# Where the transposed loads of x stand on SyncE's queue, and what TensorE does between K's first pieces

## The chip, the cores and the metric

One NeuronCore of a Trainium2 chip runs the whole kernel. The metric is the device time of one execution in microseconds (us), as the median of several runs. Beside it stands one profiled execution, whose trace gives every instruction's start and duration.

## The reference, cut to what matters

x is 2048 x 640 in bf16. A gate mixes a linear-attention block with an MLP whose first layer shifts channels along the sequence:

```
q, k, v = split(x @ wqkv)                       # 32 heads of 20
phi(t)  = where(t > 0, t + 1, exp(t)) + 1e-6
a  = (phi(q) @ (phi(k)^T v)) / (phi(q) . sum_s phi(k) + 1e-6) @ wo
h  = gelu(layernorm(x) @ w1)                    # four groups of channels shifted by 1, -1, 2, -2
x1 = x + shifted(h) @ w2
b  = x1 + gelu(layernorm(x1) @ w3) @ w4
g  = sigmoid(sum(x * gate_w))
out = g * a + (1 - g) * b
```

## The kernel before, in words

The order on every engine is the order of the program text (a manual schedule); the framework only adds the semaphore waits. The 2048 rows of x are 16 chunks of 128 rows; the 640 columns are five blocks of 128 (index dc). The stages follow one another on TensorE: K for each chunk (L185), Q in ten units (L242), the product of phi(k) and x (L319), the layers of the MLP and the attention output.

K of a chunk needs xT, x transposed, in SBUF, as the weights of ten matmuls (five blocks dc, two halves of the output), and wk, the K columns of wqkv. Chunks 0 and 1 are transposed on TensorE: turn(c) (L207) multiplies x by an identity into PSUM (L215 for chunk 0, L213 for chunk 1), and VectorE copies the result to xT (L218), blocks 0 and 1 first, then 2 to 4. Chunks 2 to 15 are transposed by DMA: load_xT (L122) issues a DMA transpose from DRAM on SyncE's queue (L123).

The gate's dot product rides along in K: wk_sb has one more column, filled with gate_w. L217 is a small matmul that turns gate_w into that layout, and L221 copies it to wk_sb. The second half of every K piece has 321 columns and reads it.

The loads are issued at the start of the program (L128 to L147). On SyncE: x chunk 0, wk blocks 1, 3 and 4, then the six transposes (chunks 2, 3, 4-5, 6-7, 8-11, 12-15), wq (L138, into the memory of hsT), the other chunks of x (L139, by L120), wv, w1, wo, w2, w3. On ScalarE: gate_w, wk block 0, x chunk 1, wk block 2. Every DMA also waits for the completion counter that it shares with the DMA eight before it.

K of chunk 0 takes its blocks in the order 1, 0, 3, 4, 2, as the wk blocks come in (k0_order, L192). warmup (L196) puts matmuls on a constant, whose results are not used, on TensorE: six while nothing has been loaded yet (L202, L203), one after turn(0) (L224), and one of 256 columns, a filler, between the first and second and between the second and third pieces of K (L229). Ahead of the fourth piece stands turn(1).

GpSimd makes the masks and the identity (L150 to L166) and then w1x, a copy of parts of w1 (L167 to L169), which waits for the load of w1. Its next work is the rstd of the layer norm (L289, L290).

Of the kernel before, what the change touches and what calls it, by code (L numbers as in the profile page):

```python
# [16 lines left out]
def kernel(  # L17
# [13 lines left out]
    nc = tc.nc  # L31
    P = 128
    S, D = A_x.shape[1], A_x.shape[2]
    F = B_w3.shape[1]
    H, Dh = 32, 20
    NCH = S // P
# [3 lines left out]
    DC = D // P  # L40
# [4 lines left out]
    CG = D // 4  # L45
# [4 lines left out]
    NG = 6  # L50
    row0 = [g * GW for g in range(5)] + [D - P]
# [3 lines left out]
    x2 = A_x.rearrange("b s d -> (b s) d")  # L55
    out2 = out.rearrange("b s d -> (b s) d")
    wqkv_v = A_wqkv.rearrange("(c p) f -> p c f", p=P)
# [20 lines left out]
    w1_sb = const.tile([P, DC, D], BF16)  # L78
    w1x = const.tile([P, DC, P], BF16)
    w2_sb = const.tile([P, DC, D], BF16)  # L80
    w3_sb = const.tile([P, DC, F], BF16)
    wo_sb = const.tile([P, NG, D], BF16)
# [21 lines left out]
    wq_sb = hsT[:, :, 0:D]  # L104
    wv_sb = m_sb
# [5 lines left out]
    xT = st1.tile([P, DC, S], BF16)  # L111
# [5 lines left out]
    sp, aq, gq = nc.sync, nc.scalar, nc.gpsimd  # L117

    def load_x(c0, c1, q=sp):
        q.dma_start(x_sb[:, c0:c1, 0:D], x2[c0 * P:c1 * P, :].rearrange("(c p) d -> p c d", p=P))  # L120

    def load_xT(c0, c1):  # L122
        sp.dma_start_transpose(xT[:, :, c0 * P:c1 * P], x2[c0 * P:c1 * P, :])  # L123

    def load_wk(q, dc):
        q.dma_start(wk_sb[:, dc, 0:D], A_wqkv[dc * P:(dc + 1) * P, D:2 * D])
# [6 lines left out]
    load_wk(sp, 3)  # L133
    load_wk(aq, 2)
    load_wk(sp, 4)
    for c0, c1 in ((2, 3), (3, 4), (4, 6), (6, 8), (8, 12), (12, 16)):
        load_xT(c0, c1)
    sp.dma_start(wq_sb, wqkv_v[:, :, 0:D])  # L138
    load_x(2, 16)  # L139
    sp.dma_start(wv_sb[:], wqkv_v[:, :, 2 * D:3 * D])  # L140
    sp.dma_start(w1_sb[:], B_w1.rearrange("(c p) f -> p c f", p=P))
    for g in range(NG):
        sp.dma_start(wo_sb[:, g, :], A_wo[row0[g]:row0[g] + P, :])
    for g in range(4):
        sp.dma_start(w2_sb[:, g, :], B_w2[CG * g:CG * g + P, :])
        sp.dma_start(w2_sb[32 * g:32 * (g + 1), 4, :], B_w2[CG * g + P:CG * (g + 1), :])
    sp.dma_start(w3_sb[:], B_w3.rearrange("(c p) f -> p c f", p=P))  # L147


    nc.gpsimd.memset(mhalf[:], -0.5)  # L150
# [10 lines left out]
    for m, n, off in ((bmask, GH, 0), (bmask5, 2, 88)):  # L161
# [2 lines left out]
                                base=-off, pattern=[[-Dh, n], [0, 4]], channel_multiplier=1)  # L164
        nc.gpsimd.affine_select(out=m[:], in_=m[:], compare_op=ALU.is_ge, fill=0.0,
                                base=off + Dh - 1, pattern=[[Dh, n], [0, 4]], channel_multiplier=-1)  # L166
    for dc in range(DC):  # L167
        for g in range(4):
            nc.gpsimd.tensor_copy(w1x[:, dc, 32 * g:32 * (g + 1)], w1_sb[:, dc, CG * g + P:CG * (g + 1)])  # L169


    def phi(dst, src, n):
# [8 lines left out]
    def k_mm(pt, c, dcs, first=0, last=DC - 1):  # L181
        for dc in dcs:
            for hf in range(2):
                n = HD + hf
                nc.tensor.matmul(pt[:, hf, 0:n], lhsT=xT[:, dc, c * P:(c + 1) * P],  # L185
                                 rhs=wk_sb[:, dc, hf * HD:hf * HD + n], start=(dc == first), stop=(dc == last))
# [9 lines left out]
    def warmup(n, w=TS):  # L196
        for i in range(n):
            nc.tensor.matmul(warm[:, 1, 0:w], lhsT=one[:, 0:P], rhs=one[:, 0:w], start=True, stop=True)  # L198
# [8 lines left out]
    def turn(c):  # L207
        for pt, a, b in turns:
            ptb = pt[:, 0, :].bitcast(BF16) if c else pt[:, 0, :]
            for dc in range(a, b):  # L210
                dst, src = ptb[:, (dc - a) * P:(dc - a + 1) * P], x_sb[:, c, dc * P:(dc + 1) * P]
                if c:
                    nc.tensor.transpose(dst, src, ident[:])  # L213
                else:
                    nc.tensor.matmul(dst, lhsT=src, rhs=ident[:], start=True, stop=True)  # L215
            if c == 0 and b == DC:
                nc.tensor.matmul(pt[:, 1, 0:DC], lhsT=g5z[:], rhs=ident[:, 0:DC], start=True, stop=True)  # L217
            nc.vector.tensor_copy(xT[:, a:b, c * P:(c + 1) * P],  # L218
                                  ptb[:, 0:(b - a) * P].rearrange("p (c s) -> p c s", c=b - a))
            if c == 0 and b == DC:  # L220
                nc.vector.tensor_copy(wk_sb[:, :, D], pt[:, 1, 0:DC])  # L221

    turn(0)
    warmup(1, TS)  # L224
    for n, dc in enumerate(k0_order):
        if n == 3:
            turn(1)
        elif 1 <= n < 3:
            warmup(1, 2 * P)  # L229
        k_mm(kp, 0, (dc,), first=k0_order[0], last=k0_order[-1])  # L230
    k_evac(kp, 0)
    for c in range(1, NCH):
# [414 lines left out]
```

## Time and profile before

| | |
|---|---|
| median of 3 runs | 263.02 us (262.87 to 264.37) |
| the profiled execution's own time | 262.89 us |
| its span, first to last instruction | 261.1 us |
| granted TensorE clock | 1.00 |
| VectorE busy in 0 to 27.2 us (K's stage) | 18.28 us |
| K: first matmul to Q's first matmul | 4.22 to 27.22 us |
| SyncE's last early load (w3) issued | 36.76 us |
| SyncE's next transpose | 54.08 us |

All times in the trace are counted from the start of the span. PE is TensorE's matmuls and PEld its weight loads, which overlap with matmuls; DVE is VectorE, ACT ScalarE, POOL GpSimd, SPq SyncE's queue of DMA issues. A DMA row's duration is the time that its issue takes on the queue, not the transfer. Matmuls are pipelined and their ends are modelled, so two rows can overlap; the distance between two starts is what a matmul costs.

### The profile page before, as it was taken

How to read it: one execution, taken by the hardware profiler on the slowest of the kernel's cores; microseconds unless marked ns; L12 is line 12 of the kernel's file. 1: busy time of each engine (PE TensorE's matmuls, PEld its weight loads, DVE VectorE, ACT ScalarE, POOL GpSimd, SP SyncE). 2: the span in 40 equal slices, each digit the busy share in tenths (PEclk: the TensorE clock that was granted, in tenths of full speed). 3: DMA queues.
4: the chain of work that ended last, by engine and by line, in shares of the span. 5: the costliest groups of instructions: out<-in, count | busy, mean ns of one | idle time of the engine just before them, and what ended most of it. 6: DMA issues, size and time to landing. Idle time of an engine off the chain costs nothing.

```text
span 261.1 us, 4172 instructions
## 1 busy us (share of the span) xinstructions
PE 257.6 (99%) x1670; PEld 159.1 (61%) x1670; DVE 141.9 (54%) x277; ACT 82.9 (32%) x124; POOL 27.1 (10%) x82
## 2 busy tenths in 40 slices
PE   8999999999999999999999999999999999999995
PEld 4777555788754644565676566567745567555543
DVE  2788778899947884967312378970312223112132
ACT  1555554321165346431520311140233350142100
POOL 3000050012220140131000123310000000000000
PEclk9999999999999999999999999999999999999999
DMA  7999987016684826996002011331200001100011
GB/s 205 179 204 377 365 241 306 0 28 126 125 99 88 220 54 145 207 298 60 0 3 75 25 28 25 75 54 25 78 25 0 0 3 50 53 0 0 0 53 50
DMA packets 47265, 25.78 MB, mean 99 GB/s; under 512 B 35214, under 2 KB 46478, under 8 KB 47246
## 3 DMA queue, kind: packets, MB, share of 16 engines
q1 hardware_dynamic: 46804, 25.03, 39.5%
q10 hardware_dynamic: 442, 0.49, 0.5%
q8 instruction: 13, 0.21, 0.4%
q14 instruction: 6, 0.05, 0.1%
HBM read 13.03 MB, written 3.60 MB: 64 GB/s over the span
## 4 chain that ended last, share of the span: by engine, by line
PE 99%; DVE 0%; issue 0%
PE pp L518 22%; PE pp L483 21%; PE pp L185 9%; PE pp L319 8%; PE pp L436 8%; PE pp L467 8%; PE pp L353 8%; PE pp L242 8%; PE pp L198 1%; PE pp L527 1%; PE pp L492 1%; PE pp L386 1%; PE pp L372 1%; PE pp L257 0%; PE pp L215 0%; DVE oc L532 0%
## 5 line engine op out<-in xcount | busy, mean ns | idle before, releaser
L483 PE MATMUL pp<-lnxT,w_sb 128*128 128x512 bf16 x260 | 60.0, 379 | 0.0
L518 PE MATMUL pp<-w_sb,h 128*128 128x384 bf16 (+3 forms) x416 | 57.9, 299 | 0.0
L485 ACT ACTIVATE h<-pp 128x1024 bf16<-128x1024 f32 (+1 forms) x28 | 27.0, 963 | 94.3 <-PE pp L483 94.3
L518 PEld LDWEIGHTS <-h 128*128 128x128 bf16 x416 | 38.3, 98 | 19.4 <-issue 1.2
L483 PEld LDWEIGHTS <-w_sb 128*128 128x128 bf16 x260 | 25.4, 98 | 27.2
L532 DVE SCALAR_TENSOR_TENSOR oc<-pp,omg,x 128x640 bf16<-128x640 f32 (+2 forms) x20 | 14.4, 748 | 45.4 <-PE pp L527 21.2
L470 DVE SCALAR_TENSOR_TENSOR x<-pp,gate,x 128x640 f32<-128x640 f32 x16 | 14.1, 879 | 33.6 <-PE pp L467 33.6
L177 ACT ACTIVATE e<-pp 128x640 bf16<-128x640 f32 (+1 forms) x26 | 21.5, 827 | 9.6 <-PE pp L242 9.6
L467 PE MATMUL pp<-m_sb,pqT 128*128 128x320 bf16 x160 | 24.3, 299 | 0.0
L436 PE MATMUL pp<-w_sb,hsT 128*128 128x320 bf16 x160 | 23.5, 299 | 0.0
L185 PE MATMUL pp<-wk_sb,xT 128*128 128x320 bf16 (+1 forms) x160 | 23.0, 302 | 0.0
L319 PE MATMUL pp<-x_sb,pk 128*128 128x320 bf16 (+1 forms) x160 | 22.0, 300 | 0.0
L242 PE MATMUL pp<-xT,hsT 128*128 128x512 bf16 x100 | 21.7, 379 | 0.0
L319 PEld LDWEIGHTS <-pk 128*128 128x128 bf16 x160 | 18.8, 117 | 3.2
L436 PEld LDWEIGHTS <-hsT 128*128 128x128 bf16 x160 | 15.6, 98 | 7.7
L467 PEld LDWEIGHTS <-pqT 128*128 128x128 bf16 x160 | 15.7, 98 | 7.7
L289 POOL TENSOR_SCALAR rstd<-mv 128x1 f32<-128x1 f32 (+1 forms) x20 | 7.7, 386 | 115.4 <-DVE mv L295 115.4
L185 PEld LDWEIGHTS <-xT 128*128 128x128 bf16 x160 | 15.6, 99 | 6.5 <-DVE xT L218 0.2
L439 DVE TENSOR_TENSOR x<-pp,x_sb 128x640 f32<-128x640 f32 x16 | 13.1, 816 | 10.6 <-PE pp L436 10.4
L353 PE MATMUL pp<-lnxT,w_sb 128*128 128x512 bf16 x80 | 18.1, 379 | 0.0
L242 PEld LDWEIGHTS <-hsT 128*128 128x128 bf16 x100 | 11.8, 118 | 9.7
L179 DVE SCALAR_TENSOR_TENSOR pk<-pp,e 128x640 bf16<-128x640 f32 x16 | 13.2, 825 | 1.7
(75 smaller groups left out, 191.1 us busy)
## 6 DMA issues: line engine op xcount, KB each, us to landing
x_sb<-in_A_x_dram SPq DMA_DIRECT2D x1, 2240.0 KB, 11.2
out_dram<-oc SPq DMA_DIRECT2D x14, 160.0 KB, 1.8
w_sb<-in_B_w_dram SPq DMA_DIRECT2D x1, 2160.0 KB
w_sb<-in_B_w_dram SPq DMA_DIRECT2D x1, 2080.0 KB, 11.7
wo_sb<-in_A_wo_dram SPq DMA_DIRECT2D x6, 160.0 KB, 7.3
m_dram<-x SPq DMA_DIRECT2D x3, 320.0 KB, 2.9
hsT<-in_A_wqkv_dram SPq DMA_DIRECT2D x1, 800.0 KB
m_sb<-in_A_wqkv_dram SPq DMA_DIRECT2D x1, 800.0 KB
```

The costliest lines, as they stand in the source:

```text
L177: nc.scalar.activation(ev, src, ACT.Exp)
L185: nc.tensor.matmul(pt[:, hf, 0:n], lhsT=xT[:, dc, c * P:(c + 1) * P], rhs=wk_sb[:, dc, hf * HD:hf * HD + n], start=(dc == first), stop=(dc ...
L242: nc.tensor.matmul(pt[:, t % 2, :], lhsT=wq_sb[:, dc, :].rearrange("p (m j) -> p j m", j=DC)[:, j], rhs=xT[:, dc, t * TS:(t + 1) * TS], st ...
L319: nc.tensor.matmul(pt[:, hf, 0:HD + hf], lhsT=w, rhs=x_sb[:, c, hf * HD:(hf + 1) * HD + hf], start=(c == 0), stop=(c == NCH - 1))
L353: nc.tensor.matmul(pt[:, i, :], lhsT=w, rhs=lnxT[t][:, dc, :], start=(dc == 0), stop=(dc == DC - 1))
L436: nc.tensor.matmul(pt[:, hf, 0:HD], lhsT=hsT[:, fc, 2 + c * P:2 + (c + 1) * P], rhs=w2_sb[:, fc, hf * HD:(hf + 1) * HD], start=(fc == 0), ...
L467: nc.tensor.matmul(pt[:, hf, 0:HD], lhsT=pqT[:, j, c * P:(c + 1) * P], rhs=m_sb[:, j, hf * HD:(hf + 1) * HD], start=(j == 0), stop=(j == D ...
L470: nc.vector.scalar_tensor_tensor(x1, pt[:, :, 0:HD], gate[:, c:c + 1], x1, op0=ALU.mult, op1=ALU.add)
L483: nc.tensor.matmul(pt[:, k, :], lhsT=w3_sb[:, dc, fc * P:(fc + 1) * P], rhs=lnT[:, dc, :], start=(dc == 0), stop=(dc == DC - 1))
L485: nc.scalar.activation(h2[:, 2 * i * TS:(2 * i + n) * TS], pt[:].rearrange("p h e -> p (h e)")[:, 0:n * TS], ACT.Gelu_apprx_tanh)
L518: nc.tensor.matmul(dst, lhsT=st[t]["h2"][:, fc * TS + cc * P:fc * TS + (cc + 1) * P], rhs=w4_sb[:, fc, a:b], start=start and fc == 0, stop ...
L532: nc.vector.scalar_tensor_tensor(oc[:, a:b], src, omg[:, c:c + 1], st[t]["x1"][cc][:, a:b], op0=ALU.mult, op1=ALU.add)
```

## The change

- The late loads (transposes, wq and all behind it) are put into a function, late_loads, which is called after turn(0) in the program text. SyncE's queue holds the same DMAs in the same order, but the transposes are now one per chunk: 14 instead of 6.
- A new memset on VectorE writes one column of xT in chunk 2, which the first transpose writes too. So the first transpose has to wait for this memset, and all later DMAs of SyncE's queue stand behind it.
- The matmul for the gate column and its copy to wk_sb move from after the second half of turn(0) to after its first half. The memset follows that copy, ahead of the second copy to xT.
- The two fillers between K's pieces are gone.
- GpSimd's copies to w1x move in the text behind late_loads, as they must follow the load of w1. GpSimd's own order stays the same.

The lines of the kernel after are shifted by a few against those of before: L198 becomes L197, L185 becomes L184, L138 becomes L140.

```diff
-    def load_xT(c0, c1):
-        sp.dma_start_transpose(xT[:, :, c0 * P:c1 * P], x2[c0 * P:c1 * P, :])
+    def load_xT(c):
+        sp.dma_start_transpose(xT[:, :, c * P:(c + 1) * P], x2[c * P:(c + 1) * P, :])
...
-    for c0, c1 in ((2, 3), (3, 4), (4, 6), (6, 8), (8, 12), (12, 16)):
-        load_xT(c0, c1)
-    sp.dma_start(wq_sb, wqkv_v[:, :, 0:D])
-    load_x(2, 16)
...
+    def late_loads():
+        for c in range(2, NCH):
+            load_xT(c)
+        sp.dma_start(wq_sb, wqkv_v[:, :, 0:D])
+        load_x(2, 16)
...
-    for dc in range(DC):
-        for g in range(4):
-            nc.gpsimd.tensor_copy(w1x[:, dc, 32 * g:32 * (g + 1)], w1_sb[:, dc, CG * g + P:CG * (g + 1)])
...
-            if c == 0 and b == DC:
+            if c == 0 and a == 0:
                 nc.tensor.matmul(pt[:, 1, 0:DC], lhsT=g5z[:], rhs=ident[:, 0:DC], start=True, stop=True)
             nc.vector.tensor_copy(xT[:, a:b, c * P:(c + 1) * P],
                                   ptb[:, 0:(b - a) * P].rearrange("p (c s) -> p c s", c=b - a))
-            if c == 0 and b == DC:
+            if c == 0 and a == 0:
                 nc.vector.tensor_copy(wk_sb[:, :, D], pt[:, 1, 0:DC])
+                nc.vector.memset(xT[:, 0:1, 2 * P:2 * P + 1], 0.0)
 
     turn(0)
+    late_loads()
+    for dc in range(DC):
+        for g in range(4):
+            nc.gpsimd.tensor_copy(w1x[:, dc, 32 * g:32 * (g + 1)], w1_sb[:, dc, CG * g + P:CG * (g + 1)])
     warmup(1, TS)
     for n, dc in enumerate(k0_order):
         if n == 3:
             turn(1)
-        elif 1 <= n < 3:
-            warmup(1, 2 * P)
         k_mm(kp, 0, (dc,), first=k0_order[0], last=k0_order[-1])
```

More of the change, by code (lines that the diff above doesn't have):

```diff
@@ L135 @@
     load_wk(sp, 4)
-    for c0, c1 in ((2, 3), (3, 4), (4, 6), (6, 8), (8, 12), (12, 16)):
-        load_xT(c0, c1)
-    sp.dma_start(wq_sb, wqkv_v[:, :, 0:D])
-    load_x(2, 16)
[L140 to L143, printed above, removed]
-    for g in range(4):
-        sp.dma_start(w2_sb[:, g, :], B_w2[CG * g:CG * g + P, :])
-        sp.dma_start(w2_sb[32 * g:32 * (g + 1), 4, :], B_w2[CG * g + P:CG * (g + 1), :])
-    sp.dma_start(w3_sb[:], B_w3.rearrange("(c p) f -> p c f", p=P))
+    def late_loads():
[3 more added lines that the diff above has]
+        load_x(2, 16)
+        sp.dma_start(wv_sb[:], wqkv_v[:, :, 2 * D:3 * D])
+        sp.dma_start(w1_sb[:], B_w1.rearrange("(c p) f -> p c f", p=P))
+        for g in range(NG):
+            sp.dma_start(wo_sb[:, g, :], A_wo[row0[g]:row0[g] + P, :])
+        for g in range(4):
+            sp.dma_start(w2_sb[:, g, :], B_w2[CG * g:CG * g + P, :])
+            sp.dma_start(w2_sb[32 * g:32 * (g + 1), 4, :], B_w2[CG * g + P:CG * (g + 1), :])
+        sp.dma_start(w3_sb[:], B_w3.rearrange("(c p) f -> p c f", p=P))
     nc.gpsimd.memset(mhalf[:], -0.5)
@@ L166 @@
                                 base=off + Dh - 1, pattern=[[Dh, n], [0, 4]], channel_multiplier=-1)
-    for dc in range(DC):
-        for g in range(4):
-            nc.gpsimd.tensor_copy(w1x[:, dc, 32 * g:32 * (g + 1)], w1_sb[:, dc, CG * g + P:CG * (g + 1)])
     def phi(dst, src, n):
@@ L219, in turn @@
                                   ptb[:, 0:(b - a) * P].rearrange("p (c s) -> p c s", c=b - a))
-            if c == 0 and b == DC:
+            if c == 0 and a == 0:
                 nc.vector.tensor_copy(wk_sb[:, :, D], pt[:, 1, 0:DC])
+                nc.vector.memset(xT[:, 0:1, 2 * P:2 * P + 1], 0.0)
     turn(0)
+    late_loads()
+    for dc in range(DC):
+        for g in range(4):
+            nc.gpsimd.tensor_copy(w1x[:, dc, 32 * g:32 * (g + 1)], w1_sb[:, dc, CG * g + P:CG * (g + 1)])
     warmup(1, TS)
```

## The prediction

> **What bounds the kernel now.** I read the page first: busy time, then the chain that ended last.
>
> ```profile
> span 261.1 us, 4172 instructions
> PE 257.6 (99%) x1670; PEld 159.1 (61%) x1670; DVE 141.9 (54%) x277; ACT 82.9 (32%) x124; POOL 27.1 (10%) x82
> ...
> PE 99%; DVE 0%; issue 0%
> ```
>
> TensorE carries the whole end. The busy time by stage says the same: 21.80 of 21.8 us in 27.2:49, and 50.00 of 50 in each of the three stages from 100 to 250. So a microsecond that TensorE gains or loses in the first 27 us reaches the end almost whole, and the change acts only there. Hence the next view, the timeline of TensorE in the first 10 us (start, duration, line; the end of a matmul is modelled, so the next start is the safer mark).
>
> ```profile
> 3.23 0.74 PE L215 MATMUL pp<-ident,x_sb 128*128 128x128 bf16 x5
> 3.77 0.21 PE L217 MATMUL pp<-ident,g5z 128*128 128x5 bf16 x1
> 3.84 0.59 PE L198 MATMUL pp<-const-bfloat16-1.0 128*128 128x512 bf16 x1
> 4.22 0.93 PE L185 MATMUL pp<-wk_sb,xT 128*128 128x320 bf16 x2
> 4.94 0.42 PE L198 MATMUL pp<-const-bfloat16-1.0 128*128 128x256 bf16 x1
> 5.15 0.48 PE L185 MATMUL pp<-wk_sb,xT 128*128 128x320 bf16 x2
> 5.47 0.27 PE L198 MATMUL pp<-const-bfloat16-1.0 128*128 128x256 bf16 x1
> 5.58 0.43 PE L185 MATMUL pp<-wk_sb,xT 128*128 128x320 bf16 x2
> 5.85 0.44 PE L213 MATMUL pp<-ident,x_sb 128*128 128x128 bf16 x5
> ```
>
> The two L198 rows at 4.94 and 5.47 are the fillers that go: they take 4.94 to 5.15 and 5.47 to 5.58, 0.32 us together. The second K matmul starts only at 4.72 (same timeline, narrower window), since it waits for the column copy of L221. After this K's fourth piece starts at 6.13 and its fifth at 6.51, though the fourth needs only 2 x 0.136: a gap of 0.11 us, which I read as the last piece of wk arriving.
>
> SyncE's queue, from its timeline:
>
> ```profile
> 2.65 13.64 SPq L123 DMA_TRANSPOSE xT<-in_A_x_dram  x6
> 16.33 0.58 SPq L138 DMA_DIRECT2D hsT<-in_A_wqkv_dram  x1
> ...
> 57.80 5.24 SPq L311 DMA_TRANSPOSE lnxT<-ln  x4
> ```
>
> And the one wait of TensorE on a transpose of x, from the waits (total, times, longest):
>
> ```profile
> PEld L185 <- DMA xT<-in_A_x_dram: 0.2, 1, 0.2
> ```
>
> The six transposes start at 2.65, 3.99, 5.30, 6.74, 8.60 and 12.72. So one chunk alone costs SyncE 1.31 to 1.34 us from start to start, two cost 1.44 to 1.86, four 4.1 and 3.6. The four of L311 give the same 1.31 each. The wait of 0.2 at 16.30 held up a weight load only.
>
> **What the skill says.** "DMA: Bandwidth & Descriptors", section on queues, rings and completion order: each DMA engine takes turns between the queues that have work, packet by packet. That is why a transpose on SyncE's queue can delay a wk piece on ScalarE's; the trace agrees in so far as the rate falls from 371 GB/s (5.0:5.5) to 282 and 149 (5.5:6.0, 6.0:6.5) while wk ends. Same page, latency and other measured facts: a DMA transpose moves 261 GB/s, so by estimate 0.63 us for a chunk of 164 KB, less than the 1.31 us that issuing it takes. The trace doesn't split the two. "TensorE: Matmul & The Clock Gate", Part 1: the full clock comes after a free-running window of about 3.4 us of activity. Here weight loads fall from 151 to 98 ns between 4.2 and 4.7 and matmul steps from 0.27 to 0.13 near 5.1, 4.3 us after the first.
>
> **The change, step by step.**
>
> *Fillers and the column.* L217 moves ahead of three transposes, its copy L221 ahead of the second copy. The first copy now also waits for L217, which starts at about 3.45 and takes 0.11: copy at about 3.70 instead of 3.69. It takes 0.43, the column then 0.17 and the new memset 0.1 (POOL's small ones and L200 take 0.10 to 0.11): column ready at 4.2 instead of 4.67, memset done at 4.3, second copy done at about 4.8 instead of 4.58. That copy is needed at the third piece only, at 5.1 at the earliest. TensorE could thus save 0.32 (fillers) and 0.2 (wait for the column), so the third piece could start at 5.1 instead of 5.58.
>
> *But wk has to be there.* x's first two chunks and five wk pieces are 7 x 164 KB = 1.15 MB. By the rates 0.53 MB move in 2:4, 0.37 in 4:5, 0.19 in 5:5.5, so the last byte comes near 5.7 if nothing shares the queues. In before the last piece was usable at 6.51, with transposes between; without them I put it at 6.1 (0.4 from byte to use). If the third piece still can't start before 5.58, third piece, second turn and fourth piece take 0.27 + 0.28 + 0.27, and the fifth starts at 6.40 instead of 6.51: gain 0.11. If all arrive as early as the bytes allow it starts at 6.1: gain 0.41. I take **-0.15**, since 5.58 follows the second filler directly and may be either.
>
> *The transposes wait.* The first is now behind the memset: about 4.35 instead of 2.65. Then 14 at 1.31 us: 18.3 us instead of 13.64. The next twelve follow on SyncE alone; each DMA also waits for the one eight before it (the listing of instructions shows eight completion counters in turn), which is long past at this pace. Landing: L311's shortest issue-to-landing is 2.6, so chunk c is there at 4.35 + 2.6 + 1.31(c - 2) = 6.95 + 1.31(c - 2). K needs it at about 8.0 + 1.365(c - 2): ScalarE's evacuations are 1.365 apart, and chunk 2 was begun at about 8.0. Slack is 1.0 us at first and grows by 0.055 a chunk: cost **0**, hidden behind K's own matmuls. Without that cover each chunk would cost pace minus 1.365.
>
> *wq behind them.* Issue at 4.35 + 18.3 = 22.7 instead of 16.33. Bytes: 819 KB at 375 GB/s (19:20 in before) is 2.2 us; first bytes about 1.1 after the issue (x's first chunk: issue 0.79, bytes from about 1.9), 0.4 to be usable: 26.4 at best. In before the rate was 134 GB/s in 18:19 and 375 from 19, so wq was there at about 21.2 to 21.5, 5 us after its issue: by that 27.7. Q's first weight load is at 27.09, less the gain 26.9. So lateness is 0 to 0.8 us, below nothing excluded as wq early is no use. The slow start in before was partly the tail of the last four-chunk transpose, which is gone: I take **+0.25**.
>
> *Queued behind wq.* x's remaining chunks, wv, w1, wo, w2 and w3 all come 6.4 us later. x is first used after 48.8 (landed at 28.2: issue 16.96 plus 11.2), so 34.6 will do. POOL's w1x copies wait for w1: 32.70 becomes about 39, done at 43, and POOL's next work is at 55.92. SyncE is done with w3 at 37.2, then 43.6; its next transpose is at 54.08. The rate slices are zero from 45.7 to 52.2, room enough for 6.4 us. Cost 0. POOL's listing keeps its order.
>
> Sum: 262.89 (the profiled execution; its span is 261.1 with 1.8 around) - 0.15 + 0 + 0.25 = 262.99. That execution is 0.13 under the median of 263.02.
>
> **Rivals.** A measurement here tells about 1% (2.6 us) from no change.
>
> *Earlier wk and wq in time* (0.16): the gains come without the loss, 0.15 to 0.5: 262.4 to 262.8. For it: no backlog of transposes ahead of wq. Against: 5 us from issue to use in before.
>
> *wq or a chunk later than reckoned* (0.11): 0.5 to 1.5 us stall: 263.4 to 264.4. For it: the DMA rate in before has holes (51 GB/s in 11:12, 42 in 15:16) while transposes run. Against: those belong to the four-chunk ones, whose issue is 4 us.
>
> *The clock rises one window later* (0.06): without fillers TensorE stands some 0.3 to 0.5 us near 5.3. If that keeps the window from counting, 3.4 us run at half speed: +1.7, 264.7. Against: before, it stood 0.3 near 3.0 and the clock still rose.
>
> *The transposes become the bound* (0.07), the one on the slow side. If one chunk costs p instead of 1.31, wq is usable at 4.35 + 14p + about 4.6; with p = 1.5 that is 29.95, 3 us after 26.9: 265.9 and over. It decides from p of about 1.48. Against: 1.31 in three places; for it: these were two in a row at the most from DRAM, never fourteen.
>
> **From this to the numbers.** The forecast (0.60) covers 262.8 to 263.4. The range 262.4 to 264.3 adds the rival below and most of the one above, some 0.85 in all. Faster by over 1%: 0.01, no case gives it; slower by over 1%: 0.07, the last rival; the rest 0.92.
>
> **What would show it.** Right: SyncE's first transpose near 4.35, starts 1.31 apart, wq's issue near 22.7; no L198 between K's pieces; K's second chunk evacuated 0.1 to 0.4 earlier (8.35 before); a wait of a Q weight load on wq of 0 to 0.8 near 27; everything after shifted as a block. Wrong: TensorE waiting on xT inside K, 0.27 us steps past 6, or a shift that is swallowed after Q.

## The result, and the profile after

The kernel after takes 264.66 us in the median of six runs (264.40 to 265.24), before 263.02, here of six too; the ratio is 1.0057, with a 95% interval of 1.0035 to 1.0080. It is slower by 0.6%, within the 1% that was called no change, but outside the range on record (262.4 to 264.3). The profiled execution took 265.24 with a span of 263.5, the longest of the six, so its differences from before are somewhat larger than those of the medians.

The page of the kernel after, its span, its busy times and the chain that ended last:

```profile
span 263.5 us, 4168 instructions
PE 257.2 (98%) x1650; PEld 159.2 (60%) x1668; DVE 141.9 (54%) x278; ACT 82.9 (31%) x124; POOL 27.0 (10%) x82
...
PE 88%; SPq 7%; DMA 2%; issue 1%; DVE 1%
```

TensorE's work is the same to within 0.4 us. What is new is in the last line: SyncE's queue and a DMA are now in the chain that sets the end. The chain in order of time, for 0 to 32 us, shows where (start, duration, what):

```profile
3.70 0.42 DVE xT L217
...
13.51 1.28 SPq L123
...
14.84 2.64 SPq L123
...
17.53 1.27 SPq L123
...
24.13 5.42 DMA hsT<-in_A_wqkv_dram
...
29.59 0.41 PE pp L244
```

From VectorE's copies the path goes over all fourteen transposes, each 1.26 to 1.30 us of issue but one of 2.64, then over wq (loaded into the memory of hsT), to Q's first matmul at 29.59, which was at 27.22 before. SyncE's transposes in the kernel after, and Q's first matmuls in the kernel before:

```profile
4.26 19.82 SPq L123 DMA_TRANSPOSE xT<-in_A_x_dram  x14
```

```profile
27.22 7.07 PE L242 MATMUL pp<-xT,hsT 128*128 128x512 bf16 x32
```

TensorE's timeline and the waits of its matmuls for the kernel after:

```profile
4.47 1.76 PE L184 MATMUL pp<-wk_sb,xT 128*128 128x320 bf16 x6
6.03 0.67 PE L212 MATMUL pp<-ident,x_sb 128*128 128x128 bf16 x5
...
17.31 11.07 PE L184 MATMUL pp<-wk_sb,xT 128*128 128x320 bf16 x80 [0.53 <-DMA xT<-in_A_x_dram]
29.59 1.71 PE L244 MATMUL pp<-xT,hsT 128*128 128x512 bf16 x6 [1.21 <-DMA hsT<-in_A_wqkv_dram]
```

```profile
PE pp L244 <- DMA hsT<-in_A_wqkv_dram: 1.2, 1, 1.2
...
PE pp L184 <- DMA xT<-in_A_x_dram: 0.5, 1, 0.5
```

The fillers are gone and K's first three pieces follow one another, but there is a wait on a chunk of xT at 17.3 and one on wq at 29.6. Where the time is lost is best seen in the starts of ScalarE's evacuations in K (timeline of ScalarE, rows of ylog), which are 1.36 to 1.37 apart when nothing waits. Those of chunks 7 and 8, before and after (in brackets, how long ScalarE had stood and for whom):

```profile
16.52 0.16 ACT L189 COPY ylog<-pp 128x1 f32<-128x1 f32 x1 [0.59 <-PE pp L185]
17.88 0.16 ACT L189 COPY ylog<-pp 128x1 f32<-128x1 f32 x1 [0.59 <-PE pp L185]
```

```profile
16.82 0.16 ACT L188 COPY ylog<-pp 128x1 f32<-128x1 f32 x1 [0.59 <-PE pp L184]
18.88 0.16 ACT L188 COPY ylog<-pp 128x1 f32<-128x1 f32 x1 [1.29 <-PE pp L184]
```

The table holds what each kernel of this study shows: the first start, the steps that are longer, the sum K lost in them, and Q's first matmul less the last evacuation (-0.20 when Q waits for nothing).

| kernel | chunk 0 | longer steps, before chunk | lost in K | Q less chunk 15 | Q's first matmul |
|---|---|---|---|---|---|
| before | 6.98 | none | 0 | -0.20 | 27.22 |
| after | 7.28 | 2.06 (8) | 0.70 | 1.17 | 29.59 |
| e1_hold_six | 7.38 | 1.68 (4), 1.82 (8) | 0.78 | -0.20 | 28.38 |
| e2_split_early | 7.08 | none | 0 | 0.03 | 27.55 |
| e3_wq_scalar | 7.13 | 4.40 (4), 0.63 to 0.69 (5 to 7, catching up), 1.83 (8), 4.23 (10), 2.30 (11) | 5.16 | -0.20 | 32.55 |
| e4_fillers_back | 7.24 | 1.99 (8), 1.41 (10) | 0.68 | 0.93 | 29.28 |
| e5_no_fillers | 8.86 | 2.32 (1) | 0.96 | -0.20 | 30.05 |
| e6_column_early | 7.08 | none | 0 | -0.20 | 27.32 |
| e7_more_rows | 7.10 | 1.87 (7) | 0.51 | 0.82 | 28.87 |
| e8_hold_pairs | 7.21 | 1.59 (2) | 0.23 | -0.20 | 27.68 |
| e9_last_pairs | 6.97 | 1.46 (4), 1.66, 1.50, 1.58, 1.54 (8 to 11) | 0.95 | -0.20 | 28.15 |
| e10_no_hold | 6.98 | none | 0 | -0.20 | 27.22 |

Before to after: 0.30 by chunk 0, 0.70 at chunk 8, 1.37 at Q. Sum 2.37, the 2.4 of the spans. In the end wq alone sets Q's start: nothing on SyncE's queue up to wq waits for K, so had K lost nothing, Q would still have waited until 29.59.

### The profile page after: what moved, and what is told of

The parts are those of the page before. It is cut to its first block, busy times and chain, and to the rows that moved or that the text cites. A ratio compares the mean times of both kernels' runs of the same rounds, so it can differ in the third digit from the quotient of the medians.

```text
span 263.5 us, 4168 instructions
## 1 busy us (share of the span) xinstructions
PE 257.2 (98%) x1650; PEld 159.2 (60%) x1668; DVE 141.9 (54%) x278; ACT 82.9 (31%) x124; POOL 27.0 (10%) x82
## 4 chain that ended last, share of the span: by engine, by line
PE 88%; SPq 7%; DMA 2%; issue 1%; DVE 1%
PE pp L520 22%; PE pp L485 21%; PE pp L321 8%; PE pp L438 8%; PE pp L469 8%; PE pp L244 8%; PE pp L355 8%; SPq L123 7%; DMA hsT<-in_A_wqkv_dram 2%; PE pp L197 1%; PE pp L529 1%; PE pp L494 1%; PE pp L388 1%; PE pp L374 1%; PE pp L259 0%
## 5 line engine op out<-in xcount | busy, mean ns | idle before, releaser
L184 PE MATMUL pp<-wk_sb,xT 128*128 128x320 bf16 (+1 forms) x160 | 23.1, 306 | 0.6 <-DMA xT<-in_A_x_dram 0.5
L184 PEld LDWEIGHTS <-xT 128*128 128x128 bf16 x160 | 15.8, 99 | 7.6 <-DMA xT<-in_A_x_dram 0.9
L177 DVE TENSOR_SCALAR e<-e 128x640 bf16<-128x640 bf16 (+1 forms) x26 | 9.5, 365 | 8.5 <-ACT e L176 7.0
```

## The experiments

Each edit is against the kernel named. Ratios are to the kernel before on the same chip, with 95% intervals.

**e10_no_hold: after without its memset.**

```diff
-                nc.vector.memset(xT[:, 0:1, 2 * P:2 * P + 1], 0.0)
```

> Edit: the kernel after without its memset, nothing else: 14 transposes of one chunk, wq behind them, no fillers, column early, but nothing holds the first transpose back. Theory F (neither the hold nor the split costs by itself; together they use up the slack of both the chunks and wq): first transpose at 2.65, wq issued near 22.0 and usable near 27.3, no wait on a chunk inside K, Q waits 0 to 0.3, time 263.1 to 263.5. Rival G (14 issues cost, held back or not): 264 or more.

Measured 263.36 (ratio 0.9999, 0.9979 to 1.0018), span 261.1. Its queue, from SyncE's timeline, and TensorE's timeline at Q:

```profile
2.65 19.09 SPq L123 DMA_TRANSPOSE xT<-in_A_x_dram  x14
21.78 0.58 SPq L140 DMA_DIRECT2D hsT<-in_A_wqkv_dram  x1
```

```profile
27.22 7.07 PE L243 MATMUL pp<-xT,hsT 128*128 128x512 bf16 x31
```

One memset less and the loss is gone: fourteen transposes, wq behind them at 21.78, and Q starts where it did before. Theory F holds on this side. wq was usable at most 5.4 us after its issue; by the times of the other kernels there is next to no room left on this queue.

**e2_split_early: before, with one transpose a chunk.**

```diff
-    for c0, c1 in ((2, 3), (3, 4), (4, 6), (6, 8), (8, 12), (12, 16)):
-        load_xT(c0, c1)
+    for c in range(2, NCH):
+        load_xT(c, c + 1)
```

> Edit: the kernel before, with 14 transposes of one chunk in place of six, where they stood, fillers kept. Theory A: 14 x 1.32 from 2.65, with one hole of 1.3 us, puts wq's issue at 22.4 instead of 16.33, it is there 5.3 later at 27.7, Q waits 0.5 to 0.7; no wait on a chunk, since each is there 1.6 us earlier than after; time 263.5 to 263.8. Rival B: the split is harmless, 263.0.

Measured 263.38 (1.0004, 0.9996 to 1.0013): no difference beyond the interval. The trace shows theory A's wait, but smaller: wq issued at 21.96, the first weight load of Q held up 0.4, Q's matmul 0.23 late by the table. The 0.5 to 0.7 expected was too much.

**e1_hold_six: after, with the six transposes of before.**

```diff
-        for c in range(2, NCH):
-            load_xT(c)
+        for c0, c1 in ((2, 3), (3, 4), (4, 6), (6, 8), (8, 12), (12, 16)):
+            load_xT(c0, c1)
```

> Edit: the kernel after, but with the six transposes of before (chunks 2, 3, 4-5, 6-7, 8-11, 12-15), held back behind the memset as after has them. Theory A (the 14 single issues put wq some 6 to 8 us later, and Q waits for it 1.4 us): wq's issue comes at about 4.3 + 13.7 = 18.0 instead of 24.13, it is there near 23.5, Q's weight load doesn't wait, time 263.0 to 263.4. Rival B (holding the transposes back is itself the loss): K waits for chunks 4 to 8, whose transposes start 1.7 us later than before, and the time stays at 264 or more.

Measured 263.78 (1.0014, 1.0004 to 1.0024), above theory A's range and below B's. wq's issue at 17.52 cost nothing at Q, as A said. But K waited for chunks 4 and 8, 0.78 in all, as B said. Both chunks are the first of a longer transpose, which K needs before the rest; as I read it, they come only with the whole of it. Both theories are at work. The profiled execution, 264.17, is the longest of the 22, so 0.78 is more than the typical loss; the medians are 0.59 apart.

**e8_hold_pairs: after, with seven transposes of two chunks.**

```diff
-        for c in range(2, NCH):
-            load_xT(c)
+        for c in range(2, NCH, 2):
+            load_xT(c, c + 2)
```

> Edit: the kernel after, with seven transposes of two chunks, held back as in after. Theory F: pairs take 1.4 to 1.9 us each, so they run ahead of K by 0.4 us a chunk and the halt at TensorE's instruction fetch is hidden; wq is issued near 16.8, Q waits 0; only the first pairs can be late, by 0 to 0.4; time 263.1 to 263.6, below the 263.8 of the held six. Rival B (holding back is the loss by itself): 264 or more.

Measured 263.53 (1.0010, 0.9991 to 1.0029). SyncE's timeline:

```profile
4.26 11.20 SPq L123 DMA_TRANSPOSE xT<-in_A_x_dram  x7
15.50 1.18 SPq L140 DMA_DIRECT2D hsT<-in_A_wqkv_dram  x1
```

The pairs are issued in 11.20 us instead of 19.82, wq goes out at 15.50, and K waits once, 0.23 for the first pair. Held back, but fast enough: nearly all is regained. It doesn't beat before.

**e9_last_pairs: after, with chunks 12 to 15 in two pairs.**

```diff
-        for c in range(2, NCH):
-            load_xT(c)
+        for c in range(2, 12):
+            load_xT(c, c + 1)
+        load_xT(12, 14)
+        load_xT(14, 16)
```

> Edit: the kernel after, with chunks 12 to 15 in two transposes of two chunks each in place of four of one. Theory A (what Q waits for is wq's place on the queue): the last four take about 3.4 us instead of 5.3, wq's issue comes at about 22.2 instead of 24.13 and is usable near 27.6; Q's wait falls from 1.2 us to 0 to 0.2, K's wait on chunk 8 stays, time 263.3 to 263.7. Rival B (holding back is the loss, wherever wq stands): no more than 0.3 under the kernel after, 264.4 or more.

Measured 264.19 (1.0034, 1.0021 to 1.0048), between the two. wq's issue at 21.71 and no wait at Q, as A said, so wq's place is what Q waits for. But then K's own waits (0.95) come to light, spread over chunks 4 and 8 to 11. In the kernel after such waits cost nothing more, since wq was later still. A was too hopeful by 0.5.

**e4_fillers_back: after, with the fillers.**

```diff
+        elif 1 <= n < 3:
+            warmup(1, 2 * P)
```

> Edit: the kernel after, with the two fillers put back between K's first pieces. Theory A (the fillers are off the matter, their room is idle waiting for wk): within 0.3 of the kernel after, 264.4 to 264.9. Rival C (without fillers TensorE's clock comes later, as the weight loads of 151 ns until 6.4 us in after show against 5.2 in before): weight loads fall to 98 ns near 5.2 again and the time falls by 0.3 or more, to 264.3 or less.

Measured 264.85 (1.0055, 1.0037 to 1.0073), no different from after. Its weight loads do fall to 0.10 us by 5.5 (in after they are at 0.15 until past 6), and chunk 0 is evacuated at 7.24 all the same, because the fourth piece starts at 6.50 although the second turn began at 5.91. By the trace's completion counters (each DMA counts up when it lands) that piece's block of wk landed only at 6.45 here, and at 5.95 in after. So rival C's early clock brings no time in this execution; with wk as early as in after it might have.

**e5_no_fillers: before without the fillers.**

```diff
-        elif 1 <= n < 3:
-            warmup(1, 2 * P)
```

> Edit: the kernel before without the two fillers, nothing else. Theory A (TensorE has room for the fillers while it waits for wk): K's chunk 0 is evacuated within 0.15 us of 6.98, time within 0.3 of before. Rival C (the fillers bring the clock forward; without them the first pieces and the second turn run cold, as in after): weight loads of about 150 ns until past 6 us, chunk 0 evacuated at 7.2 to 7.4, time up by 0.2 to 0.4.

Measured 263.20 against 263.32 (ratio 1.0008, 0.9991 to 1.0024). In the median the fillers are worth nothing that can be measured, as A said. The profiled execution is another matter: it took 265.70 with a mean granted clock of 0.992. TensorE's timeline, and its stages (the last three columns are the granted clock, the DMA share and the rate):

```profile
6.76 0.43 PE L185 MATMUL pp<-wk_sb,xT 128*128 128x320 bf16 x2 [1.48 <-DMA wk_sb<-in_A_wqkv_dram]
```

```profile
8.00:9.00 1.00, 1.00 (x6) 0.57 (x4) 0.00 (x0) 0.14 (x2) 0.00 (x0) 0.50 1.29 255
9.00:10.00 1.00, 1.00 (x6) 0.53 (x5) 0.33 (x1) 0.62 (x2) 0.00 (x0) 0.50 0.80 179
```

Here wk came late, TensorE stood for 1.48 us ahead of the third piece, and then the clock, which had been full from 3.8, fell back to half from 7.2 to 10.6. Q began at 30.05. This is close to what the prediction's third rival feared (3.4 us at half speed), by a loss of the clock and not by a late rise. Seven of the 118 executions without fillers (after, e1 and e5 to e10; e3, which stood long for its own reasons, is left out) took 265.65 to 266.25 at a mean clock of 0.992 or 0.993: three here, two each in e8 and e10. None of the 133 with fillers that ran beside the experiments (before, e2, e4) was under 0.999. Only this one of the seven was profiled, so that the fillers keep the clock up is likely, but not shown.

**e6_column_early: before without fillers, with the column's matmul and copy early.**

```diff
-            if c == 0 and b == DC:
+            if c == 0 and a == 0:
```

> Edit: the kernel before without the fillers and with the gate column's matmul and copy after the first half of the turn, as after has them; no memset, so the transposes aren't held back. Theory A: the third piece still waits for wk, chunk 0 evacuated between 6.7 and 7.0 if the clock is up by 5.2, 262.7 to 263.1. Rival C: as cold as after, evacuated near 7.2, 263.2 to 263.5.

Measured 263.13 (0.9995, 0.9987 to 1.0003). Chunk 0 is evacuated at 7.08, and its third piece waits 0.47 for wk:

```profile
4.21 0.86 PE L185 MATMUL pp<-wk_sb,xT 128*128 128x320 bf16 x4
5.55 0.43 PE L185 MATMUL pp<-wk_sb,xT 128*128 128x320 bf16 x2 [0.47 <-DMA wk_sb<-in_A_wqkv_dram]
```

The first two pieces are over by 5.1 and the time that the fillers and the column had taken is now spent waiting. The column's earlier copy and the missing fillers neither help nor hurt. The clock was up early here without fillers, so C does not hold in this execution; e5 shows one in which the clock was lost.

**e7_more_rows: after, with 23 short warm-up matmuls for six long ones.**

```diff
-    warmup(5)
-    warmup(1, 3 * P)
+    warmup(23, P)
```

> Edit: the kernel after, with the six warm-up matmuls ahead of the first turn (2944 columns) replaced by 23 of 128 columns (2944 columns): 17 more weight loads and 17 more matmuls in TensorE's program at about the same time spent. Theory D (the transpose at 14.84 takes 2.64 instead of 1.28 because TensorE's instructions are fetched by DMA at 14.9): K runs through the same places of its program 34 rows, or 1.7 chunks, earlier, so the fetch moves to about 12.6 and the long issue to the 7th or 8th transpose (12.19 or 13.51). Rival E (it belongs to the ninth transpose, its ring or its counter): it stays at 14.84.

Measured 265.59 (1.0085, 1.0070 to 1.0100). The long issue is now the eighth, at 13.52 (2.13 us), and the ninth starts late, at 15.70. The queue view for 13.3 to 13.4 us shows an instruction fetch by DMA there:

```profile
q8 instruction: 1, 0.02, 79.4%
```

Rival E falls: the ninth transpose is not special. But the fetch moved by 1.6 us (14.9 in after, 13.3 here) and not by the 2.3 of theory D, and in e10_no_hold, with after's matmuls in the same order on TensorE, it was at 18.3, beside an issue of 1.91 at 18.51. So the halt goes with a fetch; whose instructions are fetched, and what places it, stays open. Part of this kernel's extra time lies elsewhere: a wait of 1.1 us on the transposes of gs (L373).

**e3_wq_scalar: after, with wq issued by ScalarE.**

```diff
-        sp.dma_start(wq_sb, wqkv_v[:, :, 0:D])
...
         k_evac(pt, c)
+        if c == 3:
+            aq.dma_start(wq_sb, wqkv_v[:, :, 0:D])
```

> Edit: the kernel after, with wq's load taken from SyncE's queue and issued from ScalarE's after the evacuation of K's chunk 3 (about 12.7 us). Theory A: wq is there by 21 at the latest, Q waits 0, time 263.2 to 263.5 (the wait on chunk 8 of 0.7 us may stay or grow by 0.3, as wq shares the DMA engines). Rival B (wq is not the cause): 264.4 to 264.8.

Measured 267.87 (1.0164, 1.0140 to 1.0188): a miss of both, by my own edit. The DMA waited for the completion counter that it shares with an earlier transpose (issued at 12.20, landed at 15.17 by that counter; wq's issue follows at 15.19), and ScalarE stood behind it; then wq and the transposes shared the DMA engines. ScalarE's timeline and TensorE's:

```profile
15.19 0.39 ACTq L238 DMA_DIRECT2D hsT<-in_A_wqkv_dram  x1
15.62 0.16 ACT L187 COPY ylog<-pp 128x1 f32<-128x1 f32 x1 [3.63 <-PE pp L183]
```

```profile
22.69 8.52 PE L183 MATMUL pp<-wk_sb,xT 128*128 128x320 bf16 x49 [1.96 <-DMA xT<-in_A_x_dram]
```

The evacuation before it was at 11.22, so a step of 4.40 us stands in K, and another of 4.23 where K waits for xT. The step of 2.30 after that ran largely at half clock (0.50 in 24:26). It says nothing on wq's place, but that moving a load to another queue is not free.

## Why the prediction was wrong, point by point

The place was right: only the first 27 us changed, and the loss there reached the end whole. The profile steps of the sum were -0.15, 0 and +0.25; they measured +0.30, +0.70 and +1.37.

**wq behind them (+0.25, measured +1.37): the term that was mis-sized.** The pace was right: 4.26 and 1.32 from start to start instead of 4.35 and 1.31. Two things were not. One of the fourteen issues took 2.64, so wq went out at 24.13 instead of 22.7. And it was usable 5.46 us after its issue, where I had counted 4.45. I held the 5 us in before to be partly the tail of a four-chunk transpose; in after, e2, e4 and e7 no such tail is ahead and it takes 5.25 to 5.6 all the same. The start is as slow: 60 GB/s in 25:26 in after and 72 in 23:24 in e10, against the 134 in 18:19 of before that I had put down to the tail. Why it is slow stays open. Together that is 2.44 later than reckoned; K's end, 1.32 later than reckoned, hid a part: 0.25 + 2.44 - 1.32 = 1.37. My upper end for this term (0.8) left out the halt.

**The transposes wait (0, measured +0.70).** By the formula chunk 8 should have been there at 14.8, and K would have begun it at 16.6. It came at 17.3. So what failed is the formula's 2.6 from issue to landing, the shortest of L311's: this transpose, issued at 12.19 on the reckoned pace, took 5.1. Two that met no halt took 2.9 (e2, e10), and two in e9 3.6 and 4.5, so the slack of 1.0 was smaller from the start. The stages of the kernel after, with the engines' busy times, then the clock, the DMA share and the rate last:

```profile
14.00:15.00 1.00, 1.00 (x10) 0.70 (x8) 0.89 (x2) 0.77 (x2) 0.00 (x0) 1.00 0.73 131
15.00:16.00 1.00, 1.00 (x10) 0.73 (x8) 0.90 (x2) 0.55 (x2) 0.00 (x0) 1.00 2.44 122
16.00:17.00 1.00, 0.78 (x6) 0.33 (x4) 0.79 (x3) 0.41 (x3) 0.00 (x0) 1.00 0.05 6
17.00:18.00 1.00, 0.69 (x5) 0.51 (x6) 0.84 (x2) 0.59 (x1) 0.00 (x0) 1.00 0.37 78
```

Almost nothing moves in 16 to 17 (6 GB/s), and packets that began in 15 to 16 last so long that the share exceeds one. The profile of before had shown the same: I quoted its 42 GB/s in 15:16 and wrote that such holes "belong to the four-chunk ones". That sentence failed. Before's queue view for 14 to 16 us has the same fetch:

```profile
q8 instruction: 1, 0.02, 3.6%
```

There the transposes ran ahead of K, and the halt cost nothing. The cover that I named, K's own matmuls, was 1.0 us plus 0.055 a chunk by my reckoning; a transfer caught in such a halt goes through it.

**Fillers, column, wk (-0.15, measured +0.30).** Without the fillers nothing is gained, since the third piece waits for wk (e6), as the bound from wk's bytes had left open. That wk would come earlier without transposes between is refuted: in the seven kernels with held transposes chunk 0 is evacuated at 6.97 to 7.38, in before, e2, e6 and e10 at 6.98 to 7.08. By the completion counters wk's last block lands at 6.42 to 6.70 in the held ones and at 6.37 to 6.48 in those four. In e4 the fourth piece waits for its block of wk (6.45); in after that block is there at 5.95 and the piece waits for the second turn, which runs at half pace until 6.5. So wk delays it in one execution and the clock in the other, and what decides between them isn't settled.

**The rivals.** The one that came true is wq or a chunk later than reckoned, at 0.11; both happened, so its 264.4 was still too low. The slow-side rival (the transposes as the bound) named the right chain but the wrong cause: the pace never left 1.32; one halt and wq's 5.46 us did it. The clock did come late in the profiled execution (second turn at 0.11 a step, past 6 us), and delays chunk 0 there; but with the clock up at 5.4 e4 takes no less time, and wq holds Q until 29.59 whatever K does, so it is not the cause of the loss. That a kernel without fillers can lose the clock for 3.4 us, e5 shows.

**What is shown.** Undoing the hold alone removes the whole loss (e10), and splitting is harmless without the hold (e2). Holding back is harmless with pairs (e8, within its interval) but not with the six, where K waits for the chunks (e1). Only both at once use up the slack of wq.

## What to carry to other kernels

A queue that issues in order has one deadline for each thing on it: add up the issues to the last item that somebody needs, and give it the same care as the first. Slack that is less than the longest halt seen anywhere in the trace is no slack, even if the halt costs nothing where it is now. Splitting transfers and delaying their start each draw on that slack; what is free alone (the split in e2) can cost a microsecond and more together with the other. And a median can hide what a trace of one execution shows: the fillers count for nothing in it, yet the clock was seen to be lost only in kernels without them.

## What the runs showed of the hardware

- On SyncE's queue a transpose of 128 x 640 from DRAM costs 1.32 us from start to start; one of two chunks takes 1.4 to 1.8 us of issue in e8. Fourteen single ones take 19.82 us (after), seven pairs 11.20 (e8).
- A load of 800 KB behind single transposes is usable 5.25 to 5.6 us after its issue (after, e2, e4, e7).
- DMA traffic nearly stops once in K; in after it is under 13 GB/s from 15.9 to 17.25 by the queue view. In seven traces of kernels with single transposes the long issue (1.91 to 2.64) begins within 0.3 us of the start of a 16 KB instruction fetch; e3 has a second one, of 2.61 at 19.91, without a fetch beside it, so the fetch is not the only occasion. That they go together is shown, that the fetch causes the halt is not.
- Weight loads fall from 151 to 98 ns anywhere from 3.4 us (e9) to 6.4 us (after) in kernels that do the same up to there. The Trainium skill's "TensorE: Matmul & The Clock Gate", Part 1, calls the window free-running; these traces agree. Its transition at about 4 us of activity, give or take 0.5, doesn't hold here: it comes 2.6 to 5.6 us after the first matmul (0.83).
- A short stand can be followed by a loss of the clock: half clock from 7.2 to 10.6 after TensorE stood for 1.48 us (e5), 0.50 in 24:26 after 1.96 us (e3). A stand of 1.21 us in after was not.
